# A decode step of cached attention and a gMLP: K transposed by the vector engine instead of the tensor engine, with other layouts for P, O and the weights

## The chip, the cores and the metric

The kernel runs on one core of a Trainium2 chip. The metric is the device time of one execution in microseconds; less is better. Before the change the median of three runs is 678.7 us (677.94 to 678.73). Profiled executions have a span that is a little shorter than the timed run (676.9 us for this one).

## The reference

One decode step with a batch of 4. The input row is normalised; its query attends to a cache of 4,096 keys and values in 32 heads of 128; beside it a gMLP branch works on the same normalised row; all is summed.

```python
B, Sq, D = (4, 1, 640)
H, Sk, Dh = (32, 4096, 128)
q = (x @ wq).reshape(B, Sq, H, Dh)                 # transposed to b h q d
scores = einsum('bhqd,bhkd->bhqk', q, k_cache) * Dh ** (-0.5)
p = softmax(scores)
o = einsum('bhqk,bhkd->bhqd', p, v_cache)
A = o.reshape(B, Sq, H * Dh) @ wo
# B branch, F = 1728, Fh = 864
z = gelu(einsum('bsd,df->bsf', x, w_in))
z1, z2 = z[..., :Fh], layernorm(z[..., Fh:])
g = w_sp * z2 + b_sp                               # S = 1
Bb = (z1 * g) @ w_out
return x0 + A + Bb                                 # x = layernorm(x0)
```

All inputs are bf16. The two caches are 4 x 32 x 4096 x 128 elements each, 134 MB, and every byte is read once: with the weights 282.2 MB come from memory.

## The kernel before, in words

Heads are taken in eight groups of four (`HG = 4`, `NG = 8`). One group of one batch element is a unit, `u` for K and `v` for V, 32 of each (`NU`). A unit is a tile of 128 partitions x 16,384 bf16, 4 MB: partition (head e, block m of 32) holds 128 consecutive keys of 128 elements, so each partition's row is 32 KB in one piece. All unit tiles come from one pool, `kvpool`, with five buffers; the two halves of `wq` and the gMLP weights use buffers of the same pool. All loads are issued in order by SP (`load_unit` at L273, `load_wo` at L281), each as soon as its buffer is free, and a load that waits holds back those behind it.

The program is one loop over steps `s` (L429), four to a unit, so that a step is a quarter of a unit (`NCH = 4`). In step `s`:

- `emit_T` (L296) transposes a quarter of K unit `u = s // 4`. K is read as words of two bf16, and TensorE transposes 16 blocks of 128 x 128 such words as f32 against the identity (L303) into PSUM tiles `pst` (three buffers). ScalarE (L292) and VectorE (L294) take turns in copying a `pst` out to `kT`.
- `emit_S` (L310) multiplies the quarter transposed one step earlier: eight matmuls of 512 columns (L321), four 32-column groups of the array side by side, one for each head, with weights from a zero-padded copy of q (`QZ`) that puts each result on its own row of the tile `S`. After 16 steps `S` of a group is full.
- Then the softmax of the group: the row maximum through small vector steps (L327 to L338), exp on ScalarE (L341), a 32x32-block transpose of P by VectorE (L349), copies by GpSimd (POOL) into the zero-padded weights `Zb` (L362, `z_fill`), and the row sums (`norm`, L366).
- `emit_V` (L375) starts `VD = 18` steps after K of the same group: 32 matmuls a V unit (L386), again in four column groups, into the PSUM tile `O`. After each two units `O` goes to SBUF (`emit_O`, L391), f32 matmuls select each head's part (`emit_sel`, L399), and after the fourth unit the group is projected with its slice of `wo` (`emit_proj`, L407, L411) into `proj`, which holds the sum over the whole kernel and starts with the input row.

`wo` of a group is a tile of 128 partitions x 4 heads x 640; a row in memory is 640 bf16, 1,280 bytes. Its pool has one buffer, so the load for the next group waits for the projection. The gMLP weights are loaded at step 28, its matmuls run at step 34 (L204 to L267); `w_out` has rows of 1,280 bytes.

The last V unit is loaded in four pieces (`TAIL`), and treated apart (L457 to L481): the earlier batch elements of the last group are projected first (L470), then 128 matmuls with V as weights (L479) give the last batch element, which is projected in turn (L481). L484 converts the sum and two stores end the kernel.

Of the kernel before, what the change touches and what calls it, by code (L numbers as in the profile page):

```python
# [16 lines left out]
def kernel(  # L17
# [16 lines left out]

    nc = tc.nc
    P = 128
# [8 lines left out]
    KP = T // (2 * NCH)  # L45
    assert KP == 16 and M == 32
# [5 lines left out]
    FC = (Fh + P - 1) // P  # L52
    FL = Fh - (FC - 1) * P
# [11 lines left out]
    ppool = ctx.enter_context(tc.tile_pool(name="ppool", bufs=1))  # L65
    opool = ctx.enter_context(tc.tile_pool(name="opool", bufs=1))
    wopool = ctx.enter_context(tc.tile_pool(name="wopool", bufs=1))
    ps_t = ctx.enter_context(tc.tile_pool(name="ps_t", bufs=3, space=bass.MemoryType.PSUM))
    ps_s = ctx.enter_context(tc.tile_pool(name="ps_s", bufs=2, space=bass.MemoryType.PSUM))
    ps_o = ctx.enter_context(tc.tile_pool(name="ps_o", bufs=1, space=bass.MemoryType.PSUM))  # L70
    ps_m = ctx.enter_context(tc.tile_pool(name="ps_m", bufs=1, space=bass.MemoryType.PSUM))
    ps_j = ctx.enter_context(tc.tile_pool(name="ps_j", bufs=1, space=bass.MemoryType.PSUM))
# [16 lines left out]
    nc.sync.dma_start(out=x_bf[:], in_=x_flat)  # L89


# [18 lines left out]
    QL = 16 + G * 32 + 16  # L110
    QZ = []
    for i in range(2):
        qz = const.tile([P, 2, QL], BF16, name=f"QZ{i}")
        nc.gpsimd.memset(qz[:].rearrange("p a l -> p (a l)").bitcast(F32), 0.0)
        QZ.append(qz)

# [25 lines left out]

    I32 = const.tile([P, 32], F32)
# [3 lines left out]
    B4 = const.tile([P, B], F32)  # L147
    nc.vector.tensor_reduce(out=B4[:], in_=I32[:].rearrange("p (w b c) -> p b w c", w=2, c=NCH), axis=AX.XY, op=ALU.add)
    SelP = const.tile([P, HG, B], F32)
    nc.vector.memset(SelP[:], 0.0)  # L150
    for q in range(4):
        nc.vector.tensor_copy(out=SelP[32 * q:32 * q + 32, q, :], in_=B4[32 * q:32 * q + 32, :])

    Pm = const.tile([P, 2, 2, P // 2], BF16)
    for w in range(2):
        nc.vector.tensor_copy(out=Pm[:, :, w, :], in_=ident_bf[:].rearrange("p (k w) -> p w k", w=2))
# [6 lines left out]
    m1 = const.tile([P, 32], F32)  # L163
    nc.vector.memset(m1[:], 0.0)
# [3 lines left out]
    for hf in range(NH):  # L168
        nc.tensor.matmul(proj[32 * hf:32 * hf + 32, 0:NO2], lhsT=ident_bf[:B, 0:32],
                         rhs=x_bf[:, hf * NO2:(hf + 1) * NO2], start=True, stop=False)  # L170

# [8 lines left out]
    q2_ps = misc_ps([P, 2, H * B], F32)  # L180
    for w in range(2):
        nc.tensor.matmul(q2_ps[:, w, :], lhsT=Pm[:, w, :, :].rearrange("p a k -> p (a k)"), rhs=q_bf[:],
                         start=True, stop=True)
    q2 = const.tile([P, 2, H * B], BF16)
    nc.vector.tensor_copy(out=q2[:], in_=q2_ps[:])

    def fill_qz(g):
        qz = QZ[g % 2]
        for w in range(2):
            r0 = 64 * w  # L190
            nc.gpsimd.tensor_copy(  # L191
                out=qz[r0:r0 + 64, :, 16:16 + G * 32].rearrange("p a (i z) -> p a i z", z=32)[:, :, :, 16 * w],
                in_=q2[r0:r0 + 64, :, g * G:(g + 1) * G])


    gw = {}
    wsp_bf = const.tile([P, 1], BF16)
    bsp_bf = const.tile([P, 1], BF16)
    wsp_f = const.tile([P, 1], F32)
    bsp_f = const.tile([P, 1], F32)  # L200
    nc.gpsimd.dma_start(out=wsp_bf[:], in_=B_w_sp.rearrange("a b -> (a b)").to_broadcast((P, 1)))
    nc.gpsimd.dma_start(out=bsp_bf[:], in_=B_b_sp.to_broadcast((P, 1)))

    def load_gmlp_weights():  # L204
        wt = kv_tile("w_gmlp")
        n_in = DC * F2
        w_in = wt[:, 0:n_in].rearrange("p (c f) -> p c f", c=DC)
        nc.sync.dma_start(out=w_in, in_=B_w_in.rearrange("(p c) f -> p c f", c=DC))
        w_out = wt[:, n_in:n_in + FC * NOUT].rearrange("p (c n) -> p c n", c=FC)
        nf = (FC - 1) * P  # L210
        nc.sync.dma_start(out=w_out[:, 0:FC - 1, :], in_=B_w_out[0:nf, :].rearrange("(c p) n -> p c n", p=P))
        nc.sync.dma_start(out=w_out[:FL, FC - 1, :], in_=B_w_out[nf:Fh, :])
        gw["in"] = w_in
        gw["out"] = w_out

    def gmlp_branch():
        nc.vector.tensor_copy(out=wsp_f[:], in_=wsp_bf[:])
        nc.vector.tensor_copy(out=bsp_f[:], in_=bsp_bf[:])
        zT = const.tile([P, 2, FC, B], F32)
        nc.vector.memset(zT[:], 0.0)  # L220
        zT_ps = misc_ps([P, 2, FC, B], F32)
        for part in range(2):
            for fc in range(FC):
                n = P if fc < FC - 1 else FL
                for c in range(DC):
                    f0 = part * Fh + fc * P
                    nc.tensor.matmul(zT_ps[:n, part, fc, :], lhsT=gw["in"][:, c, f0:f0 + n],  # L227
                                     rhs=xnT[:, c, :], start=(c == 0), stop=(c == DC - 1))
        nc.scalar.activation(out=zT[:, :, 0:FC - 1, :], in_=zT_ps[:, :, 0:FC - 1, :], func=ACT.Gelu_apprx_tanh)
        nc.scalar.activation(out=zT[:FL, :, FC - 1, :], in_=zT_ps[:FL, :, FC - 1, :], func=ACT.Gelu_apprx_tanh)  # L230
        z1 = zT[:, 0, :, :]
        z2 = zT[:, 1, :, :]
        st_in = const.tile([P, 2, FC, B], F32)
        nc.vector.tensor_copy(out=st_in[:, 0], in_=z2)
        nc.vector.tensor_tensor(out=st_in[:, 1], in0=z2, in1=z2, op=ALU.mult)
        st_ps = misc_ps([P, 2, FC, B], F32)
        nc.tensor.matmul(st_ps[:].rearrange("p s c b -> p (s c b)"), lhsT=ones_f[:, :],
                         rhs=st_in[:].rearrange("p s c b -> p (s c b)"), start=True, stop=True)
        st = const.tile([P, 2, B], F32)
        nc.vector.tensor_reduce(out=st[:], in_=st_ps[:].rearrange("p s c b -> p s b c"), axis=AX.X, op=ALU.add)  # L240
        mean = const.tile([P, B], F32)
        nc.vector.tensor_scalar(out=mean[:], in0=st[:, 0, :], scalar1=1.0 / Fh, scalar2=None, op0=ALU.mult)
        msq = const.tile([P, B], F32)
        nc.vector.tensor_tensor(out=msq[:], in0=mean[:], in1=mean[:], op=ALU.mult)
        var = const.tile([P, B], F32)
        nc.vector.scalar_tensor_tensor(out=var[:], in0=st[:, 1, :], scalar=1.0 / Fh, in1=msq[:],
                                       op0=ALU.mult, op1=ALU.subtract)
        rs = const.tile([P, B], F32)
        nc.scalar.activation(out=rs[:], in_=var[:], func=ACT.Sqrt, bias=eps_t[:, 0:1], scale=1.0)
        nc.vector.reciprocal(out=rs[:], in_=rs[:])  # L250
        t1 = const.tile([P, FC, B], F32)
        nc.vector.tensor_tensor(out=t1[:], in0=z2, in1=mean[:, None, :].to_broadcast((P, FC, B)),
                                op=ALU.subtract)
        nc.vector.tensor_tensor(out=t1[:], in0=t1[:], in1=rs[:, None, :].to_broadcast((P, FC, B)),
                                op=ALU.mult)
        nc.vector.tensor_scalar(out=t1[:], in0=t1[:], scalar1=wsp_f[:, 0:1], scalar2=bsp_f[:, 0:1],
                                op0=ALU.mult, op1=ALU.add)
        uT = const.tile([P, FC, B], BF16)
        nc.vector.tensor_tensor(out=uT[:], in0=z1, in1=t1[:], op=ALU.mult)
        gw["uT"] = uT  # L260

    def gmlp_out():
        for fc in range(FC):
            n = P if fc < FC - 1 else FL
            for hf in range(NH):
                nc.tensor.matmul(proj[32 * hf:32 * hf + B, 0:NO2], lhsT=gw["uT"][:n, fc, :],
                                 rhs=gw["out"][:n, fc, hf * NO2:(hf + 1) * NO2], start=False, stop=False)  # L267


    wo_v = A_wo.rearrange("(h p) n -> p h n", p=P)  # L270
    state = {}
# [9 lines left out]
    def load_wo(g):  # L281
        wo_t = wopool.tile([P, HG, NOUT], BF16, tag="wo", name=f"wo{g}")
        nc.sync.dma_start(out=wo_t[:], in_=wo_v[:, g * HG:(g + 1) * HG, :])
        state[("wo", g)] = wo_t

    evac_ctr = [0]

    def evacuate(dst, src):
        k = evac_ctr[0] % 2
        evac_ctr[0] += 1  # L290
        if k:
            nc.scalar.copy(out=dst, in_=src)  # L292
        else:
            nc.vector.tensor_copy(out=dst, in_=src)  # L294

    def emit_T(u, ch):  # L296
        kw = state[("k", u)][:].bitcast(F32)
        kT = ktpool.tile([P, KP, HG, M, 2], BF16, tag="kT", name="kT")
        for pc in range(4):
            pst = ps_t.tile([P, 4, P], F32, tag="pst", name="pst")  # L300
            for e in range(4):
# [115 lines left out]
    def at(s, fn):  # L417
        sched.setdefault(s, []).append(fn)
# [98 lines left out]
```

## Time and profile before

| | before |
|---|---|
| time, median of 3 | 678.7 us |
| span of the profiled run | 676.9 us |
| PE busy | 501.5 us (74%) |
| of it K transposes, L303 | 313.1 us |
| ACT busy, of it copies of K, L292 | 275.0 us, 254.9 us |
| DVE busy, of it copies of K, L294 | 218.4 us, 176.9 us |
| bytes read, mean rate | 282.24 MB, 417 GB/s |
| a 4 MB tile of K, issue to landing | 43.6 us |

The busy times are sums over an engine's instructions; engines run side by side, so they don't add up. The page cuts the span into 40 slices and gives for each the busy share of an engine in tenths, the share of the DMA engines and the rate. The time from issue to landing is long because several tiles are queued at a time: it is a queue's length, not a transfer's.

### The profile page before, as it was taken

How to read it: one execution, taken by the hardware profiler on the slowest of the kernel's cores; microseconds unless marked ns; L12 is line 12 of the kernel's file. 1: busy time of each engine (PE TensorE's matmuls, PEld its weight loads, DVE VectorE, ACT ScalarE, POOL GpSimd, SP SyncE). 2: the span in 40 equal slices, each digit the busy share in tenths (PEclk: the TensorE clock that was granted, in tenths of full speed). 3: DMA queues.
4: the chain of work that ended last, by engine and by line, in shares of the span. 5: the costliest groups of instructions: out<-in, count | busy, mean ns of one | idle time of the engine just before them, and what ended most of it. 6: DMA issues, size and time to landing. Idle time of an engine off the chain costs nothing.

```text
span 676.9 us, 10603 instructions
## 1 busy us (share of the span) xinstructions
PE 501.5 (74%) x4663; PEld 356.0 (53%) x4663; DVE 218.4 (32%) x398; ACT 275.0 (41%) x291; POOL 33.5 (5%) x92
## 2 busy tenths in 40 slices
PE   0699898669766797677687787688876789766846
PEld 0566566446544565555465556456654556554424
DVE  4144542243222433223233242233332243322300
ACT  0176764364423544334344333344442444433300
POOL 1000200010000010002000020000100010000100
PEclk9999998788878989688898878987787998967865
DMA  8999999999999999999999999999999999999994
GB/s 324 431 429 429 433 423 429 407 430 432 416 429 431 431 433 417 429 434 431 429 419 433 427 431 428 422 433 432 429 417 431 431 429 433 423 425 432 409 417 171
DMA packets 15333, 282.92 MB, mean 418 GB/s; under 512 B 1356, under 2 KB 6328, under 8 KB 6584
## 3 DMA queue, kind: packets, MB, share of 16 engines
q1 hardware_dynamic: 15216, 282.25, 98.0%
q8 instruction: 36, 0.59, 0.4%
q14 instruction: 9, 0.07, 0.0%
q0 software_dynamic: 64, 0.00, 0.0%
q10 hardware_dynamic: 8, 0.00, 0.0%
HBM read 282.24 MB, written 0.01 MB: 417 GB/s over the span
## 4 chain that ended last, share of the span: by engine, by line
DMA 58%; PE 32%; ACT 6%; DVE 3%; issue 1%; SPq 0%; ACTq 0%; DVEq 0%
DMA k<-in_A_k_cache_dram 55%; PE pst L303 19%; PE S L321 5%; ACT kT L292 4%; PE O L386 3%; DMA v<-in_A_v_cache_dram 3%; PE misc L403 1%; PE proj L411 1%; DVE kT L294 1%; ACT p_bf L341 1%; PE ol L479 1%; DVE m L327 1%; DVE x L349 0%; PE misc L368 0%; PE misc L227 0%
## 5 line engine op out<-in xcount | busy, mean ns | idle before, releaser
L292 ACT COPY kT<-pst 128x1024 bf16<-128x1024 bf16 x256 | 254.9, 1013 | 325.9 <-PE pst L303 243.3
L303 PE MATMUL pst<-ident_f,k 128*128 128x128 f32 x2048 | 313.1, 310 | 99.9 <-DMA k<-in_A_k_cache_dram 95.2
L303 PEld LDWEIGHTS pst<-ident_f,k 128*128 128x128 f32 x2048 | 265.9, 160 | 164.0 <-issue 122.2
L294 DVE COPY kT<-pst 128x1024 bf16<-128x1024 bf16 x256 | 176.9, 692 | 334.9 <-PE pst L303 321.1
L321 PE MATMUL S<-kT,QZ 128*32 128x512 bf16 x1024 | 95.2, 385 | 13.0 <-ACT kT L292 9.9
L386 PE MATMUL O<-v,Zb 128*32 128x512 bf16 x992 | 67.4, 411 | 10.1 <-DMA v<-in_A_v_cache_dram 10.1
L386 PEld LDWEIGHTS <-Zb 128*32 128x32 bf16 x992 | 31.0, 101 | 39.0 <-issue 15.3
L321 PEld LDWEIGHTS <-QZ 128*32 128x32 bf16 x1024 | 20.9, 94 | 49.8 <-issue 38.0
L362 POOL COPY Zb<-x 32x256 bf16<-32x256 bf16 x64 | 25.2, 394 | 184.0 <-DVE ds L351 153.5
L403 PE MATMUL misc<-I,O_sb 128*128 128x8 f32 x120 | 20.2, 296 | 9.4 <-DVE O_sb L294 6.3
L403 PEld LDWEIGHTS misc<-I,O_sb 128*128 128x128 f32 x120 | 19.0, 241 | 14.8 <-DVE O_sb L294 10.7
L191 POOL COPY QZ<-q 64x32 bf16<-64x32 bf16 x16 | 5.1, 320 | 422.6 <-PE S L321 402.4
L294 DVE COPY O_sb<-O 128x512 f32<-128x512 f32 x8 | 5.5, 692 | 36.8 <-PE O L386 36.8
L368 PE MATMUL misc<-ds,ones_f 128*128 128x16 f32 x16 | 3.6, 302 | 13.6 <-DVE ds L351 13.3
L462 ACT COPY O_sb<-O 128x512 f32<-128x512 f32 x1 | 0.6, 585 | 28.0 <-PE O L386 28.0
L341 ACT ACTIVATE p_bf<-S,negmax 128x512 bf16<-128x512 f32 x8 | 5.5, 687 | 15.9 <-DVE negmax L338 15.8
L368 PEld LDWEIGHTS misc<-ds,ones_f 128*128 128x128 f32 x16 | 2.9, 225 | 16.8 <-DVE ds L351 16.3
L404 DVE TENSOR_TENSOR oT<-misc,rinv 128x8 bf16<-128x8 f32 x15 | 2.5, 167 | 28.0 <-PE misc L403 28.0
L176 PE MATMUL misc<-xnT,wq 128*128 128x4 bf16 x160 | 4.6, 166 | 8.2 <-DMA wq<-in_A_wq_dram 4.5
L411 PE MATMUL proj<-wo,oT 128*4 128x320 bf16 x64 | 8.8, 420 | 2.1 <-DVE oT L404 1.8
L176 PEld LDWEIGHTS <-wq 128*128 128x128 bf16 x160 | 4.4, 104 | 8.4 <-DMA wq<-in_A_wq_dram 8.4
L349 DVE STREAM_TRANSPOSE x<-p_bf 128x512 bf16<-128x512 bf16 x8 | 5.7, 712 | 9.7 <-ACT p_bf L341 9.7
(88 smaller groups left out, 74.5 us busy)
## 6 DMA issues: line engine op xcount, KB each, us to landing
k<-in_A_k_cache_dram SPq DMA_DIRECT2D x32, 4096.0 KB, 43.6
v<-in_A_v_cache_dram SPq DMA_DIRECT2D x31, 4096.0 KB, 37.5
wo<-in_A_wo_dram SPq DMA_DIRECT2D x8, 640.0 KB, 29.3
wq<-in_A_wq_dram SPq DMA_DIRECT2D x1, 3072.0 KB
w_gmlp<-in_B_w_in_dram SPq DMA_DIRECT2D x1, 2160.0 KB, 31.8
wq<-in_A_wq_dram SPq DMA_DIRECT2D x1, 2048.0 KB
v<-in_A_v_cache_dram SPq DMA_DIRECT2D x1, 2048.0 KB, 23.5
v<-in_A_v_cache_dram SPq DMA_DIRECT2D x1, 1024.0 KB, 25.5
```

Of the source, the lines that this page charges most:

```text
L176: nc.tensor.matmul(q_ps[:, h, :], lhsT=wq_t[c][:, h * Dh:(h + 1) * Dh], rhs=xnT[:, c, :], start=(c == 0), stop=(c == DC - 1))
L292: nc.scalar.copy(out=dst, in_=src)
L294: nc.vector.tensor_copy(out=dst, in_=src)
L303: nc.tensor.transpose(pst[:, e, :], kw[:, k * P:(k + 1) * P], ident_f[:])
L321: nc.tensor.matmul(S_ps[32 * hd:32 * hd + 32, :, :], lhsT=qz[:, w, w0:w0 + 32], rhs=kT[:, :, hd, :, w], start=(b == 0 and ch == 0 and w == 0),
L327: nc.vector.tensor_reduce(out=m1[:, 0:1], in_=S_ps[:].rearrange("p k m -> p (k m)"), axis=AX.X, op=ALU.max)
L341: nc.scalar.activation(out=p_bf[:].rearrange("p k m -> p (k m)"), in_=S_ps[:].rearrange("p k m -> p (k m)"), func=ACT.Exp, bias=negmax[:, ...
L362: nc.gpsimd.tensor_copy(out=dst, in_=x[r0:r0 + 32, :, 2 * bb:2 * bb + 2, :])
L386: nc.tensor.matmul(O_ps[32 * q:32 * q + 32, :, :], lhsT=Zb[bb][:, w0:w0 + 32], rhs=vv[:, e, :, :], start=(b1 == 0 and e < 4), stop=((b1 == ...
L403: nc.tensor.matmul(oh[:], lhsT=O_sb[:, j, :], rhs=SelO[:, j, :, :], start=(j == 0), stop=(j == 3))
L411: nc.tensor.matmul(proj[32 * hf:32 * hf + B, 0:NO2], lhsT=oT[:, hd, :], rhs=wo_t[:, hd, hf * NO2:(hf + 1) * NO2], start=False, stop=(last ...
L479: nc.tensor.matmul(ol_ps[:], lhsT=vv[:, t, :], rhs=zc, start=(t == 0), stop=(t == T - 1))
```

## The change

Its purpose is to take the transposes of K from TensorE and their copies from ScalarE and VectorE, and to give loads longer rows. The parts:

1. K: VectorE's own transpose, which turns each 32 x 32 block of 4-byte words on its own, from SBUF to SBUF (`emit_T`). `kT` holds other pieces of the key dimension on each block of 32 partitions, so that `emit_S` has four matmuls for each of two column groups, and q is brought to a matching layout (`Pm`, `q3`, `fill_qz`).
2. P: the maximum is spread by an f32 matmul with ones; exp writes each value four times; 16 TensorE transposes bring P into PSUM; ScalarE fills `Zb` from there (GpSimd before).
3. O: always copied by ScalarE; selected once a group, with eight f32 matmuls that have O as the moving operand, a mask and four small matmuls (`emit_sel`, `emit_oT`). The last group keeps the old way and is projected once, at the end.
4. `wo` of the first seven groups is read with the four rows of a partition in one piece (5,120 bytes), and loaded seven steps later; groups 5 and 6 in three pieces by partitions. The last group's `wo` keeps its rows, comes in three pieces, and is issued just ahead of the last V tile.
5. The gMLP weights are the first load and the gMLP is computed before q. `w_out` lies on 108 partitions with eight rows of 640 in one piece each. The input row is loaded from ScalarE's queue.

```diff
+    wg = kv_tile("w_gmlp")
+    nc.sync.dma_start(out=w_in, in_=B_w_in.rearrange("(p c) f -> p c f", c=DC))
+    w_out = wg[:FP, n_in:n_in + FC * NOUT].rearrange("p (c n) -> p c n", c=FC)
+    nc.sync.dma_start(out=w_out, in_=B_w_out.rearrange("(p c) n -> p c n", c=FC))
...
+    wo_q = A_wo.rearrange("(g p c) n -> g p c n", p=P, c=HG)
...
     def emit_T(u, ch):
         kw = state[("k", u)][:].bitcast(F32)
-        kT = ktpool.tile([P, KP, HG, M, 2], BF16, tag="kT", name="kT")
-        for pc in range(4):
-            pst = ps_t.tile([P, 4, P], F32, tag="pst", name="pst")
-            for e in range(4):
-                k = ch * KP + pc * 4 + e
-                nc.tensor.transpose(pst[:, e, :], kw[:, k * P:(k + 1) * P], ident_f[:])
-            evacuate(kT[:, pc * 4:(pc + 1) * 4].rearrange("p e h m w -> p (e h m w)"),
-                     pst[:].rearrange("p e m -> p (e m)").bitcast(BF16))
+        n = TC * KW
+        kT = ktpool.tile([P, n], F32, tag="kT", name="kT")
+        nc.vector.transpose(kT[:], kw[:, ch * n:(ch + 1) * n])
...
-        for w in range(2):
-            for hd in range(HG):
-                w0 = 16 + (hd * B + b) * 32 - (b * NCH + ch)
-                nc.tensor.matmul(S_ps[32 * hd:32 * hd + 32, :, :], lhsT=qz[:, w, w0:w0 + 32],
-                                 rhs=kT[:, :, hd, :, w], start=(b == 0 and ch == 0 and w == 0),
-                                 stop=(b == B - 1 and ch == NCH - 1 and w == 1))
+        for kw in range(4):
+            for i in range(2):
+                q = 2 * (ch % 2) + i
+                nc.tensor.matmul(S_ps[32 * q:32 * q + 32, :, :], lhsT=qz[:, b, kw, w0:w0 + 32],
+                                 rhs=kT[:, i, :, kw // 2, :, kw % 2], start=(b == 0 and c2 == 0 and kw == 0),
+                                 stop=(b == B - 1 and c2 == 1 and kw == 3))
...
+            p_i = opool.tile([P, 8, HG, M], BF16, tag="O_sb", name="p", bufs=3)
+            nc.scalar.activation(out=p_i[:], in_=S_ps[:, 8 * i:8 * i + 8, None, :].to_broadcast((P, 8, HG, M)),
+                                 func=ACT.Exp, bias=negmax[:, 0:1], scale=scale, accum_out=rs2[:, i:i + 1])
...
-        nc.vector.transpose(x[:].rearrange("p e b c -> p (e b c)"), p_bf[:].rearrange("p k m -> p (k m)"))
+        for t in range(16):
+            nc.tensor.transpose(x[:, t, :], p_bf[t // 8][:, t % 8].rearrange("p h m -> p (h m)"), IdP[:])
...
-            nc.gpsimd.tensor_copy(out=dst, in_=x[r0:r0 + 32, :, 2 * bb:2 * bb + 2, :])
+                nc.scalar.copy(out=dst, in_=src[:, 2 * bb + b1])
...
+    WO_CUTS = {NG - 3: (0, 112, 120, 128), NG - 2: (0, 112, 124, 128)}
...
-        at(NCH * B * g + VD + 4, lambda g=g: load_wo(g))
+        at(min(NCH * B * g + VD + 11, NCH * (NU - 1) + VD), lambda g=g: load_wo(g, WO_CUTS.get(g, (0, P))))
```

## The prediction

> **What bounds the kernel now.** I read the page's occupancy first, then the DMA queues, then the stretches of the span, and the chain of waits last. The 40 slices say which resource never rests:
>
> ```profile
> PE 501.5 (74%) x4663; PEld 356.0 (53%) x4663; DVE 218.4 (32%) x398; ACT 275.0 (41%) x291; POOL 33.5 (5%) x92
> DMA  8999999999999999999999999999999999999994
> DMA packets 15333, 282.92 MB, mean 418 GB/s; under 512 B 1356, under 2 KB 6328, under 8 KB 6584
> q1 hardware_dynamic: 15216, 282.25, 98.0%
> q8 instruction: 36, 0.59, 0.4%
> ```
>
> No compute engine is full; the DMA engines are at nine tenths or more in every slice but the first and the last. The chain of waits gives PE 32% of the span and the L303 transposes 19%, which invites the reading that PE is half the bound. It isn't: in the first 90 us PE runs nearly without a break and the DMA share is still 1.0, because five tiles of `kvpool` let the queue run ahead. So the removal of PE transposes is worth nothing by itself; what counts is bytes times rate, plus the head, plus the tail. Stretches of 10 us (PE, PEld, DVE, ACT, POOL busy; then clock, DMA share, GB/s):
>
> ```profile
> 30.00:40.00 10.00, 10.00 (x74) 8.28 (x72) 4.82 (x8) 6.93 (x7) 0.00 (x0) 1.00 1.02 437
> 130.00:140.00 10.00, 10.00 (x71) 7.58 (x70) 4.79 (x7) 6.32 (x8) 0.00 (x0) 0.85 1.06 398
> 180.00:190.00 10.00, 9.45 (x95) 6.63 (x97) 4.48 (x7) 7.08 (x7) 0.00 (x0) 0.96 1.00 411
> 500.00:510.00 10.00, 9.77 (x83) 7.41 (x82) 5.27 (x8) 7.46 (x8) 0.00 (x0) 0.91 0.98 406
> 590.00:600.00 10.00, 2.88 (x35) 2.06 (x28) 0.88 (x3) 0.00 (x0) 0.00 (x0) 0.69 1.02 439
> ```
>
> The rate is the same with PE full (437) and PE mostly idle (439). It falls only where rows of 1,280 bytes pass: 130 to 140 holds `w_out` of the gMLP, the other two hold a `wo`. The mean of the undisturbed middle is about 428 GB/s, so one K or V tile (4096 KB = 4.194 MB) takes 9.80 us. The tail:
>
> ```profile
> 640.00:641.00 1.00, 0.90 (x12) 0.50 (x16) 0.04 (x1) 0.00 (x0) 0.74 (x2) 0.50 0.69 295
> 641.00:642.00 1.00, 1.00 (x16) 0.41 (x12) 0.00 (x0) 0.00 (x0) 0.00 (x0) 0.50 0.53 229
> 666.00:667.00 1.00, 1.00 (x6) 1.00 (x6) 0.00 (x0) 0.00 (x0) 0.00 (x0) 0.50 0.49 201
> ...
> 661.06 3.60 PE L386 MATMUL O<-v,Zb 128*32 128x512 bf16 x32 [5.32 <-DMA v<-in_A_v_cache_dram]
> 667.54 1.23 PE L411 MATMUL proj<-wo,oT 128*4 128x320 bf16 x8 [0.26 <-DVE oT L468]
> 668.70 3.57 PE L479 MATMUL ol<-Zb,v 128*128 128x4 bf16 x128
> 673.80 0.48 DVE L484 CAST o_bf<-proj 64x320 bf16<-64x320 f32 x1 [1.33 <-PE proj L411]
> ```
>
> Three losses show. At 640 to 642 the queue was nearly dry, since SP had waited up to 29.7 us for L411 to free the single `wo` buffer (the waits of the DMA queue). From 665 to 669.5 only half of the engines move data (share 0.40 to 0.57, nothing after). And the last PE work runs from V30's landing at 661.06 without a DMA wait to 672.27, some 2.5 us after the transfers stopped.
>
> [...] 712 ns for 512 elements (L349) and 212 ns for 32 (L329, f32) are 1.04 ns per element. A long f32 one isn't shown. [...] No view shows single engines. [...] matmuls into different 32-column groups run together; here eight S matmuls of 385 ns take 0.55 us at full clock, so four at a time do.
>
> **The change part by part.**
>
> K transposes. Out go 2048 PE transposes (313.1 us), 256 ACT copies (254.9) and 256 DVE copies (176.9); in come 128 DVE transposes of 128x2048 f32. From the slope: 0.212 + 2016 x 1.04 ns = 2.31 us each, 296 us in all. If 4-byte words cost two cycles it is 0.212 + 2016 x 2.08 ns = 4.4 us, 563 us. I take 2.31[...]. Need: in the K-only start a chunk arrives every 9.80/4 = 2.45 us, later every 4.9 us. At 2.31 (2.4 with gaps) DVE keeps pace even with the start; before, units 0 to 4 took 61 us, 12.2 us each, and the DMA did not notice. On the path: 0.
>
> S. Still eight matmuls per chunk, but two column groups alternate in place of four: four rounds of about 0.22 us at full clock, 0.43 at the half clock that idle stretches show, so 0.9 to 1.7 us per chunk; with V's 0.45 to 0.9, at most 2.6 of 4.9 us. If pairs did not overlap it were 3.4 + 0.9 = 4.3 us. Hidden behind the transfers either way.
>
> Softmax, Z fill, O. The chain gets longer: two exps of 1024 elements (0.69 us for 512 now, so about 1.1 each), 16 PE transposes, eight ACT copies of about 0.3 us in place of four POOL copies of 0.39, three more DVE steps. About 8 us from the maximum to Z in place of 4.5. In that time V's first matmuls and all behind them on PE wait, and ACT holds O's eviction behind the Z copies; the buffers absorb 8 us (K lands 43.6 us after issue, four tiles deep). O selection per group: 8 f32 matmuls per group for 16. All hidden, 0.
>
> Rows of 5 KB. Deficit of a window with a `wo`: (428-411)/428 x 10 = 0.40 us, 0.51 for 406. About 0.46 x 7 = 3.2 us if all comes back; [...]the eighth `wo` keeps 1,280-byte rows. I take 2.5 (range 1.5 to 3.2).
>
> gMLP first. Its row deficit was (428-398)/428 x 10 = 0.7 us[...] Net 0[...]. The order itself hides: K0 lands some 5 us later, but bytes are only reordered; K2's buffer is free near 28 us while K0 and K1 keep the queue busy to about 43. `x_bf` moves to the ACT queue: the first big load is issued 0.4 us earlier.
>
> Wo later. SP now waits for the projection behind V30, not V29, so the 640 dip (0.31 + 0.47 = 0.8 us) goes.
>
> Tail. The last group is projected once (8 matmuls, 1.23 us gone), and V31 now ends after `wo`, 1.6 us after V30 plus its own 9.8. PE's chain from V30 (3.6 + 0.6 + 1.9 + 0.2, then 3.1 us for 112 of 128 L479) is done before the last piece lands. So the end is last landing + 0.45 + 0.2 + 1.25 + 0.5 + the store of 2.6 = 5.0 us plus waits, against 676.9 - 669.5 = 7.4 now. I take 1.7 us.
>
> Balance. The half of the engines that lags carries about 4.5 us more. Instruction fetch is one suspect: 0.4% of 16 engines is 2.7 us on each, 5.4 if only eight carry it. [...] Perfect balance gives 4.5/2 = 2.2 us, none gives 0[...]. I take 1.2.
>
> Sum: 2.5 + 0 + 0.4 + 0.8 + 1.7 + 1.2 = 6.6 us. 678.7 - 6.6 = 672.1, rounded to 672.
>
> **The rivals.**
> A. The balance does not come and 5 KB rows give the low end: 1.5 + 0.4 + 0.8 + 1.0 = 3.7 us, 675.0. For it: nothing here shows which engines lag. Against: the `wo` dips are plain.
> B. All comes back and the engines end together: 3.2 + 0.4 + 0.8 + 2.2 + 2.2 = 8.8, 669.9; with both head gaps gone too (share 0.12 and 0.30 from 7 to 9 us) 668.3. For it: the share of 0.5 in the tail. Against: the head gap is unexplained.
> C. The f32 transpose is at half rate. At 4.4 + 0.1 us per chunk a unit takes 18 us, the five buffers run out between K6 and the first V tiles, and following tile by tile with five buffers the queue idles about 16 us; 672 + 16 = 688. After that 18 plus a softmax is just under the 19.6 us of a K and a V. [...]
> D. Nothing: [...]678.
>
> **How the numbers follow.** Main forecast 0.42, A 0.22, B 0.18, C 0.11, D 0.07. The range is 666.5 to 678: it holds the main case, A and B with the ends of their terms, and half of D; C stays out. Faster needs less than 677.3: the first three, 0.82; within 0.2%: most of D, 0.05; slower: C and the rest of D, 0.13.
>
> **What would show it.** Right: 128 f32 transposes near 2.3 us and DVE near 340 us busy; ACT below 80; DMA share still 0.98 or more; no dips below 415 GB/s in the middle; no dip before the last `wo`; the last PE work waiting for V31 and the end about 5.5 us after it. Wrong: a transpose of 4 us or more, a DMA share under 0.9 between 60 and 130 us (C); half the engines still moving for 4 us at the end (A); a rate in the middle other than 428, which I hold to be a property of the transfers and not of PE's traffic.

## The result, and the profile after

The change made the kernel slower: 684.25 us median (681.85 to 685.0, four runs) against 678.32 us for the kernel before in the same session (677.93 to 678.73), a ratio of 1.0081 with a 95% interval of 1.0055 to 1.0108. The profiled execution has a span of 682.6 us. The forecast of 672.0 us was wrong in direction, and the time lies above its range.

The page of the kernel after, its occupancy, DMA queues and the line of the K transposes (instruction count, tile, number | busy us, mean ns | idle time before, what ended it):

```profile
PE 341.2 (50%) x2793; PEld 152.4 (22%) x2793; DVE 318.9 (47%) x251; ACT 60.3 (9%) x183; POOL 10.2 (1%) x42
DMA  8999999999999999999999999999999999999994
GB/s 255 437 430 429 429 431 432 428 434 429 434 429 430 430 430 433 432 425 431 433 433 422 431 433 434 431 426 429 432 435 432 322 431 429 430 423 316 432 418 185
DMA packets 11916, 282.66 MB, mean 414 GB/s; under 512 B 1400, under 2 KB 1924, under 8 KB 3076
q1 hardware_dynamic: 11808, 282.25, 98.3%
q8 instruction: 22, 0.36, 0.2%
L305 DVE STREAM_TRANSPOSE kT<-k 128x2048 f32<-128x2048 f32 x128 | 284.2, 2279 | 213.8 <-DMA k<-in_A_k_cache_dram 211.4
```

All compute engines are well under full, the bytes are the same, and the DMA engines are as busy as before (98.3%, 98.0% before). Yet the mean rate fell from 418 to 414 GB/s. The slices of 17 us say where: 255 at the start (324 before), 322 and 316 late. All other slices before the last dip are 422 to 437. The engines are busy and move less, so here their packets are slower (2,038 ns against 1,215, below), and their idle time is not longer. Stretches of 10 us of the same kernel show it (PE, PEld, DVE, ACT, POOL busy; then clock, DMA share, GB/s):

```profile
10.00:20.00 10.00, 1.85 (x14) 2.04 (x14) 4.67 (x11) 1.58 (x2) 0.00 (x0) 1.00 0.98 303
520.00:530.00 10.00, 6.99 (x58) 2.91 (x56) 5.04 (x3) 0.00 (x0) 0.00 (x0) 0.75 0.98 421
530.00:540.00 10.00, 0.00 (x0) 0.00 (x0) 0.48 (x1) 0.00 (x0) 0.00 (x0) 0.59 1.03 257
540.00:550.00 10.00, 5.81 (x32) 1.62 (x31) 8.81 (x5) 0.00 (x0) 0.00 (x0) 0.73 0.99 416
610.00:620.00 10.00, 2.80 (x40) 1.95 (x40) 0.30 (x1) 0.00 (x0) 0.00 (x0) 0.86 1.03 319
620.00:630.00 10.00, 2.23 (x10) 0.61 (x12) 4.90 (x3) 0.00 (x0) 0.00 (x0) 0.50 1.00 342
```

At 530 to 540 the DMA share is 1.03 and the rate 257; PE has nothing to do, for its next tile is late. Against 428 GB/s the five late stretches lack 0.16 + 4.0 + 0.3 + 2.5 + 2.0 = 9.0 us of transfer. The timeline of SP's queue names what was in it (start, duration, load, number of pieces):

```profile
493.22 1.13 SPq L295 DMA_DIRECT2D wo<-in_A_wo_dram  x3
...
575.42 1.20 SPq L295 DMA_DIRECT2D wo<-in_A_wo_dram  x3
```

These are the two `wo` in three pieces (`WO_CUTS`). A K tile lands a median of 46.8 us after its issue, so they pass at about 535 and 620 us, in the two dips. The dip of 10 to 20 us is where `w_out` on 108 partitions passes (its packets run from 8.6 to 16.1 us). The single packets that the trace keeps, which no view prints, say the same from below: a 32 KB packet of a K or V tile takes a median of 1,215 ns from 500 to 520 us and 2,038 ns from 530 to 540; a 5,120-byte packet of `wo` takes 199 ns in the five loads that are not cut and 340 ns in the two that are. So the cut load is slow, and so are the tiles that pass beside it. The end of the chain of waits, and then three stretches of the tail (columns as above):

```profile
610.33 45.85 DMA v<-in_A_v_cache_dram
656.19 21.38 DMA v<-in_A_v_cache_dram
677.62 0.60 PE ol L520 x16
678.47 1.25 PE proj L447 x8
679.74 0.48 DVE o_bf L525
```

```profile
672.00:673.00 1.00, 0.52 (x14) 0.42 (x15) 0.17 (x1) 0.00 (x0) 0.00 (x0) 0.50 0.55 225
674.00:675.00 1.00, 0.52 (x20) 0.43 (x17) 0.00 (x0) 0.00 (x0) 0.00 (x0) 0.50 0.35 143
676.00:677.00 1.00, 0.71 (x21) 0.54 (x18) 0.00 (x0) 0.00 (x0) 0.00 (x0) 0.50 0.08 33
```

The last PE work now follows the last landing of V31 at 677.6, and the span ends 5.0 us later. The trickle is still there: a DMA share of 0.55 at 672 us, 0.35 at 674, 0.08 at 676.

### The profile page after: what moved, and what is told of

Read it like the earlier page. It is cut to its first block, busy times and chain, and to the rows that moved or that the text cites. A ratio compares the mean times of both kernels' runs of the same rounds, so it can differ in the third digit from the quotient of the medians.

```text
span 682.6 us, 6424 instructions
## 1 busy us (share of the span) xinstructions
PE 341.2 (50%) x2793; PEld 152.4 (22%) x2793; DVE 318.9 (47%) x251; ACT 60.3 (9%) x183; POOL 10.2 (1%) x42
## 3 DMA queue, kind: packets, MB, share of 16 engines
q1 hardware_dynamic: 11808, 282.25, 98.3%
## 4 chain that ended last, share of the span: by engine, by line
DMA 56%; PE 15%; issue 13%; DVE 13%; ACT 3%; POOL 0%; DVEq 0%; ACTq 0%; POOLq 0%
DMA k<-in_A_k_cache_dram 44%; DMA v<-in_A_v_cache_dram 10%; DVE kT L305 9%; PE O L409 5%; PE S L323 3%; PE zT_ps L212 2%; ACT p L351 2%; DMA bsp_bf<-in_B_b_sp_dram 2%; PE misc L426 1%; PE x L364 1%; DVE m L330 1%; PE misc L253 1%; DVE om L429 1%; PE misc L334 1%; ACT O_sb L417 0%
## 5 line engine op out<-in xcount | busy, mean ns | idle before, releaser
L305 DVE STREAM_TRANSPOSE kT<-k 128x2048 f32<-128x2048 f32 x128 | 284.2, 2279 | 213.8 <-DMA k<-in_A_k_cache_dram 211.4
L323 PE MATMUL S<-kT,QZ 128*32 128x512 bf16 x1024 | 195.4, 520 | 266.2 <-DVE kT L305 263.8
L323 PEld LDWEIGHTS <-QZ 128*32 128x32 bf16 x1024 | 55.9, 112 | 402.4 <-issue 387.3
L409 PE MATMUL O<-v,Zb 128*32 128x512 bf16 x992 | 88.0, 451 | 8.4 <-DMA v<-in_A_v_cache_dram 8.4
L351 ACT ACTIVATE p<-S,negmax 128x1024 bf16<-128x1024 f32 x16 | 17.7, 1110 | 282.3 <-DVE negmax L345 282.3
L375 ACT COPY Zb<-x 32x128 bf16<-32x128 bf16 x128 | 27.3, 254 | 10.2 <-PE x L364 9.5
L364 PE MATMUL x<-IdP,p 128*128 128x128 bf16 x128 | 16.1, 305 | 18.9 <-ACT p L351 18.6
L426 PE MATMUL misc<-O_sb,SelG 128*16 128x128 f32 x112 | 18.7, 314 | 3.7 <-ACT O_sb L417 1.5
L212 PEld LDWEIGHTS <-w_gmlp 128*108 128x108 bf16 x80 | 16.0, 294 | 0.1
L212 PE MATMUL zT_ps<-xnT,w_gmlp 128*108 128x4 bf16 x80 | 15.9, 336 | 0.3 <-DVE xnT L142 0.3
L426 PEld LDWEIGHTS misc<-O_sb,SelG 128*16 128x16 f32 x112 | 11.0, 108 | 10.3 <-ACT O_sb L417 4.0
## 6 DMA issues: line engine op xcount, KB each, us to landing
k<-in_A_k_cache_dram SPq DMA_DIRECT2D x32, 4096.0 KB, 46.8
```

The source lines that it names most:

```text
L212: nc.tensor.matmul(zT_ps[:, part, fc, :], lhsT=w[:, c, fc, :], rhs=xnT[:, c, :], start=(c == 0), stop=(c == DC - 1))
L305: nc.vector.transpose(kT[:], kw[:, ch * n:(ch + 1) * n])
L323: nc.tensor.matmul(S_ps[32 * q:32 * q + 32, :, :], lhsT=qz[:, b, kw, w0:w0 + 32], rhs=kT[:, i, :, kw // 2, :, kw % 2], start=(b == 0 and c ...
L351: nc.scalar.activation(out=p_i[:], in_=S_ps[:, 8 * i:8 * i + 8, None, :].to_broadcast((P, 8, HG, M)), func=ACT.Exp, bias=negmax[:, 0:1], s ...
L364: nc.tensor.transpose(x[:, t, :], p_bf[t // 8][:, t % 8].rearrange("p h m -> p (h m)"), IdP[:])
L375: nc.scalar.copy(out=dst, in_=src[:, 2 * bb + b1])
```

## The experiments

The theory formed from these views: a load that covers fewer than 128 partitions (its height, below; such a load is called low) is slow, and makes the transfers of its time slow (P or P1 in the expectations). The rivals: the cut loads use too few engines or load some of them more (balance, the prediction's own idea; P2); more and smaller transfers cost, whatever their shape; the vector transposes disturb the transfers. Ratios below are to the kernel before in the same session, with 95% intervals. Its median was 677.97 to 678.70 us in the four sessions, so a difference between runs of two sessions is good to some 0.7 us.

**1. The cuts of `wo` undone.**

```diff
-    WO_CUTS = {NG - 3: (0, 112, 120, 128), NG - 2: (0, 112, 124, 128)}
+    WO_CUTS = {}
```

> The changed kernel with every wo of groups 0 to 6 in one load of 128 partitions; nothing else differs. Theory P (loads of fewer than 128 partitions are slow, and slow the tiles in flight with them): the two stretches at 257 and at 319 to 342 GB/s lost (430-257)/430 x 10 = 4.0 us and (111+88)/430 x 10 = 4.6 us, so 8.6 us come back: 684.25 - 8.6 = 675.6 us, and no stretch of 10 us in the middle lies below 415 GB/s. Rival C (the vector transposes or the S matmuls hold up the transfers): the dips stay, 684 us. Rival W (5 KB rows are slow in themselves): small dips at every wo, and no gain, 683 to 684.

Measured: 675.77 us, 0.996 [0.9947, 0.9973]: 8.5 us less than the changed kernel, close to the 9.0 read from the windows. The slices of this run have the late dips gone, the one at the start not:

```profile
GB/s 251 434 424 426 433 435 434 428 427 429 436 436 425 432 427 431 436 428 429 431 430 434 431 425 434 435 426 432 431 431 434 423 432 431 434 431 428 429 417 181
```

The cuts alone turn a kernel a little faster than the one before into a slower one.

**2. The cuts in two pieces.** 112 and 16 partitions, two counts that the author assumed to give every engine the same bytes. No view shows whether they do.

```diff
-    WO_CUTS = {NG - 3: (0, 112, 120, 128), NG - 2: (0, 112, 124, 128)}
+    WO_CUTS = {NG - 3: (0, 112, 128), NG - 2: (0, 112, 128)}
```

> The changed kernel with groups 5 and 6 of wo in two pieces, 112 and 16 partitions[...]. Theory P1[...]: the dips stay, about 257 to 340 GB/s for 10 us each, 682 to 685 us. Theory P2 (what is slow is that a few engines get more than others and run out of step): the dips go, 675.6 us as without cuts.

Measured: 684.89 us, 1.01 [1.0085, 1.0115], as slow as the changed kernel. The stretches where the two loads pass:

```profile
530.00:540.00 10.00, 0.00 (x0) 0.00 (x0) 0.00 (x0) 0.00 (x0) 0.00 (x0) 0.61 1.04 277
620.00:630.00 10.00, 2.34 (x12) 0.66 (x14) 5.01 (x3) 0.00 (x0) 0.00 (x0) 0.50 0.96 331
```

So the loss needs no piece of 4, 8 or 12 partitions. That an uneven share of bytes isn't the cause either rests on the author's assumption alone.

**3. `w_out` on 96 partitions.** On top of 1.

```diff
-    FC = next(c for c in range(1, Fh + 1) if Fh % c == 0 and Fh // c <= P)
+    FC = next(c for c in range(1, Fh + 1) if Fh % c == 0 and Fh // c <= P and Fh // c % 16 == 0)
```

> No cuts of wo, and w_out on 96 partitions with nine rows each in place of 108 with eight[...]. The first 20 us moved 5.6 MB where the kernel before moved 6.8 MB, 2.9 us of transfers. Theory P2: the head comes back, 2 to 3 us less than without cuts alone, 672.7 us[...]. Theory P1: 96 partitions are still less than 128, so the head stays slow, within 1 us of the kernel without cuts, 675 to 676 us.

**4. `w_out` on 128 partitions**, six rows in one piece each, and a second small load of the 96 rows that remain; the gMLP's matmuls and tiles follow the new split (`...`). On top of 1.

```diff
...
-    nc.sync.dma_start(out=w_out, in_=B_w_out.rearrange("(p c) n -> p c n", c=FC))
+    nf = (FC - 1) * P
+    nc.sync.dma_start(out=w_out[:, 0:FC - 1, :], in_=B_w_out[0:nf, :].rearrange("(p c) n -> p c n", c=FC - 1))
+    nc.sync.dma_start(out=w_out[:FL, FC - 1, :], in_=B_w_out[nf:Fh, :])
...
```

> No cuts of wo, and w_out as 128 partitions with six rows each in one piece (960 KB) and a rest of 96 rows of 1,280 bytes (120 KB). Both P1 and P2: the head comes back, 2 to 3 us less than without cuts alone, 672.7 us, and the stretch from 10 to 20 us is above 400 GB/s in place of 303. Rival H (the slow head is the order of the loads, or the small loads of w_sp and b_sp, and not the shape of w_out): no change, 675.6 us.

Measured: 674.44 us, 0.9946 [0.9929, 0.9963] for 3, and 669.44 us, 0.987 [0.9855, 0.9884] for 4. The same stretch at the start in runs 1, 3 and 4, one fence each:

```profile
10.00:20.00 10.00, 2.06 (x15) 2.25 (x15) 4.67 (x11) 1.58 (x2) 0.00 (x0) 1.00 1.00 303
```

```profile
10.00:20.00 10.00, 2.87 (x21) 3.03 (x21) 4.66 (x11) 1.58 (x2) 0.00 (x0) 1.00 1.02 330
```

```profile
10.00:20.00 10.00, 3.84 (x74) 3.88 (x75) 4.58 (x11) 1.58 (x2) 0.00 (x0) 1.00 1.03 414
```

108 partitions 303 GB/s, 96 partitions 330, 128 partitions 414. The step from 108 to 96 gives 1.3 us, a little more than height alone was expected to give and less than balance was, if 96 partitions are the balanced load that the author took them for, which is not shown; run 4 gives 6.3, over twice the 2 to 3 expected. Of those 6.3 us the windows show (414 - 303) / 428 x 10 = 2.6 at the start, while `w_out` passes. Another 2.6 lie between 20 and 640 us, after it has landed: there run 4 moves 268.09 MB and run 1 266.97. The last 1.1 is left for the end. The part in the middle comes with the edit (266.95 MB in run 3; 268.12 and 268.04 in runs 9 and 10, which are built on run 4), but no low load is in flight then, and run 4 changes the rows' length and the gMLP's tiles along with the height. Its cause is open.

**5. Rows of 5 KB alone.** The kernel before, with `wo` of all eight groups read as the change does (so its rows no longer meet their own heads: the right output projection is left out, its work stays).

```diff
...
-        nc.sync.dma_start(out=wo_t[:], in_=wo_v[:, g * HG:(g + 1) * HG, :])
+        nc.sync.dma_start(out=wo_t[:], in_=wo_q[g])
```

> The kernel before with one edit: each partition of wo takes four neighbouring rows in one piece of 5 KB (all eight groups). The rows then meet the wrong elements of O, so this kernel leaves the right output projection out and only its time counts. The prediction's term: 2.5 us for seven loads is 0.36 us each, so 2.9 us for eight, 675.4 us; from 2 to 3.7 us, 674.6 to 676.3. Rival: rows make no difference to the end, since other losses take their place, 678 us.

Measured: 676.55 us, 0.9972 [0.9962, 0.9983], 1.4 us less by the medians and 1.2 to 2.6 by the interval. Three stretches of the run:

```profile
130.00:140.00 10.00, 10.00 (x79) 7.15 (x77) 4.89 (x8) 6.85 (x8) 0.00 (x0) 0.92 1.05 394
180.00:190.00 10.00, 9.45 (x79) 7.26 (x81) 4.59 (x7) 7.08 (x7) 0.00 (x0) 0.86 1.01 431
500.00:510.00 10.00, 9.23 (x93) 6.50 (x96) 4.85 (x7) 7.46 (x8) 0.00 (x0) 0.98 1.00 427
```

The windows of `wo` rose from 411 and 406 to 431 and 427, as forecast; that of the gMLP, which this run leaves alone, did not. But eight such dips at 0.46 us are 3.7 us, and the time fell by 1.4: what two windows of 10 us show can't be multiplied by eight.

**6. The vector transposes alone.** The kernel before with K transposed by VectorE, the PE transposes and copies gone; `emit_S` then reads blocks that it wasn't written for, so the scores are left out in effect while its work stays.

```diff
...
-                nc.tensor.transpose(pst[:, e, :], kw[:, k * P:(k + 1) * P], ident_f[:])
-            evacuate(kT[:, pc * 4:(pc + 1) * 4].rearrange("p e h m w -> p (e h m w)"),
-                     pst[:].rearrange("p e m -> p (e m)").bitcast(BF16))
+        n = KP * P
+        nc.vector.transpose(kT[:].rearrange("p k h m w -> p (k h m w)").bitcast(F32), kw[:, ch * n:(ch + 1) * n])
```

> The kernel before with one edit: each quarter of K is transposed by one vector transpose of 128x2048 f32 into kT, and the 16 PE transposes with their four copies are gone; S, then, is made of other elements, so the scores are left out and only the time counts. The prediction's term for this part: 0, so 677.5 to 679 us; at most the dry queue near the end (0.8 us) goes. Rival C: the transposes by PE and the copies by ACT and DVE were in the way of the transfers, so the time falls by more than 2 us, below 676.3. Rival D: the vector transposes slow the transfers, above 680.

Measured: 675.52 us, 0.9958 [0.9945, 0.997]: 2.5 us less. The expected 0 missed, and the time lies below rival C's 676.3. The vector transposes do not disturb the transfers; something is gained with the PE transposes and their copies gone, and run 12 asks what. Its tail, and its instruction queue, stand beside those of run 12 below.

**7. The cut at 64.** On top of 4: `wo` of the same two groups in two halves of 64 partitions.

```diff
-    WO_CUTS = {}
+    WO_CUTS = {NG - 3: (0, 64, 128), NG - 2: (0, 64, 128)}
```

> The kernel with w_out on 128 partitions (669.4 us), and wo of groups 5 and 6 in two halves of 64 partitions. [...] P1: dips for these two groups again, smaller or as large as with 112 and 16, so 672 to 678 us. Rival P3 (only counts that are no power of two, or no multiple of 32, are slow): no dip, 669.4 us.

**8. The cut in the kernel before**, without any vector transpose and with rows of 1,280 bytes.

```diff
-        nc.sync.dma_start(out=wo_t[:], in_=wo_v[:, g * HG:(g + 1) * HG, :])
+        cuts = (0, 112, 128) if g in (NG - 3, NG - 2) else (0, P)
+        for p0, p1 in zip(cuts[:-1], cuts[1:]):
+            nc.sync.dma_start(out=wo_t[p0:p1], in_=wo_v[p0:p1, g * HG:(g + 1) * HG, :])
```

> The kernel before with wo of groups 5 and 6 in two pieces of 112 and 16 partitions, rows of 1,280 bytes as they were. P1: the cut alone costs about 4 us a group here too, 683 to 688 us, with two stretches of 10 us below 350 GB/s, though PE transposes K. Rival: the cut is slow only beside the vector transposes or only with long rows, 678 to 679 us.

**10. The same number of pieces, cut by columns.** On top of 4: two loads of 128 partitions and two rows each in place of one.

```diff
-            for p0, p1 in zip(cuts[:-1], cuts[1:]):
-                nc.sync.dma_start(out=wo_t[p0:p1], in_=wo_q[g, p0:p1])
+            cc = (0, 2, HG) if g in (NG - 3, NG - 2) else (0, HG)
+            for c0, c1 in zip(cc[:-1], cc[1:]):
+                nc.sync.dma_start(out=wo_t[:, c0:c1, :], in_=wo_q[g, :, c0:c1, :])
```

> The kernel with w_out on 128 partitions, and wo of groups 5 and 6 in two loads as in the cut at 64, but cut by columns: each load has all 128 partitions, with pieces of 2,560 bytes. P1: nothing happens, 669.0 to 670.0 us and no dip, against the 678.85 us of the cut at 64 partitions. Rival Q (two loads in place of one, or one more wait in SP's queue, cost the 4 to 5 us a group): 678 us and dips.

Measured: 678.85 us for 7, 1.0013 [1.0002, 1.0024], 9.4 us above run 4, with a wider spread than the others (677.28 to 682.9 in 20 runs). 688.26 us for 8, 1.0149 [1.0134, 1.0165], 10.3 us above the kernel before. 669.3 us for 10, 0.9864 [0.985, 0.9877], no more than run 4. The stretches where the two loads pass, of 7, of 8 and of 10:

```profile
530.00:540.00 10.00, 3.48 (x16) 0.93 (x16) 6.15 (x3) 0.00 (x0) 0.00 (x0) 0.50 0.99 332
...
610.00:620.00 10.00, 0.00 (x0) 0.00 (x0) 0.69 (x1) 0.00 (x0) 0.00 (x0) 0.61 1.00 247
```

```profile
500.00:510.00 10.00, 9.68 (x83) 7.26 (x82) 5.26 (x8) 7.60 (x8) 0.00 (x0) 0.93 1.01 279
510.00:520.00 10.00, 3.59 (x48) 2.01 (x47) 0.86 (x2) 0.41 (x1) 0.00 (x0) 0.93 1.01 352
...
590.00:600.00 10.00, 8.42 (x94) 5.27 (x92) 3.64 (x7) 4.12 (x5) 0.00 (x0) 1.00 1.03 316
```

```profile
530.00:540.00 10.00, 6.55 (x30) 1.78 (x31) 8.89 (x4) 0.00 (x0) 0.00 (x0) 0.50 1.04 445
...
610.00:620.00 10.00, 5.31 (x30) 1.62 (x31) 8.89 (x4) 0.00 (x0) 0.00 (x0) 0.69 1.01 434
```

Read together: a cut by partitions costs 4 to 5 us each, at 112/16 and at 64/64, with rows of 5 KB and of 1,280 bytes, with vector transposes and without. A cut by columns costs nothing. So it is neither the number of loads, nor their row length, nor the transposes: it is that each load covers fewer than 128 partitions.

**9. `w_out` with no low load at all.** On top of 4: the second load takes the last 128 rows; the activations that meet the 32 rows which came already are set to zero (`...`).

```diff
-    nc.sync.dma_start(out=w_out[:FL, FC - 1, :], in_=B_w_out[nf:Fh, :])
+    nc.sync.dma_start(out=w_out[:, FC - 1, :], in_=B_w_out[Fh - P:Fh, :])
...
```

> The kernel with w_out on 128 partitions, and its rest taken as the last 128 rows in place of the last 96: 32 rows come twice, and their activations are set to zero the second time. No load but the input row is then on fewer than 128 partitions. P1: the rest of the dip in the stretch from 10 to 20 us (414 GB/s against 436 before) goes, 0.3 to 1 us less: 668.4 to 669.1. Rival: that dip is the eighth part of the weights in rows of 1,280 bytes, or noise, no change, 669.4 us.

Measured: 669.04 us, 0.9861 [0.9847, 0.9874]. The same stretch at the start:

```profile
10.00:20.00 10.00, 3.20 (x68) 3.24 (x69) 4.58 (x11) 1.58 (x2) 0.00 (x0) 1.00 1.02 433
```

414 became 433, the full rate, though this load reads 41 KB more; in time it is 0.4 us, within what these runs can tell. Runs 4, 9 and 10 are the fastest kernels of this study.

**11. Instructions put back, first try.** Run 6 with 16 matmuls of one column a quarter on constant operands, their result thrown away (scores left out as in 6): do the 2.5 us of run 6 come from fewer instructions being fetched?

```diff
...
+        idle = ps_t.tile([P, 16], F32, tag="idle", name="idle")
+        for e in range(16):
+            nc.tensor.matmul(idle[:, e:e + 1], lhsT=ident_bf[:], rhs=ident_bf[:, e:e + 1], start=True, stop=True)
```

> The kernel before with vector transposes of K (675.5 us), and 16 idle matmuls of one column a quarter, so that PE has as many instructions as the kernel before again: the instruction queue goes from 0.33 back to about 0.59 MB, while PE stays mostly idle and nothing waits for these matmuls. The scores are left out as there. Theory I (fewer instructions to fetch, carried by engines that finish last, gave most of the 2.5 us): 676.6 to 677.8 us. Rival J (it was the earlier issue of wo near the end, or the head): no change, 675.5 us.

Measured: 714.55 us, 1.0531 [1.0517, 1.0546]. It decides nothing between the two theories, for it made a bound of its own. Nothing held these matmuls back, so the program's order ran most of them early, ahead of q and of the first S:

```profile
70.00:80.00 10.00, 9.22 (x248) 7.50 (x246) 2.31 (x1) 0.00 (x0) 0.00 (x0) 1.00 0.01 3
```

248 matmuls in 10 us, one K transpose, and 3 GB/s: with S late, `kT` stays taken (VectorE waits up to 27.5 us for S), K's tiles don't come free, and SP has no buffer to load into (it waits up to 43.0 us for a K transpose). It shows on the way what a late S would have cost.

**12. Instructions put back, second try.** The added matmuls read the fresh `kT`, so that none can run ahead, and start with the ninth unit.

```diff
...
+        if u >= 2 * B:
+            idle = ps_t.tile([P, 20], F32, tag="idle", name="idle")
+            for e in range(20):
+                nc.tensor.matmul(idle[:, e:e + 1], lhsT=ident_bf[:], rhs=kT[:, e % KP, e % HG, 0:1, 0], start=True, stop=True)
```

> The kernel with K transposed by the vector engine alone (scores left out as in the run it is built on, 675.5 us) with 20 matmuls of one column a quarter of a unit put back on PE from the ninth unit on, each reading the fresh kT, so that none can run ahead; their result is thrown away. 24 x 4 x 20 = 1920 instructions bring PE's count near that of the kernel before; PE stays under full. Theory I, that fetching instructions costs the 2.5 us which the transposes alone gave: the instruction queue goes back to 0.5 MB or more and the time to 677.5 to 678.5 us. Theory J, that the 2.5 us come from the earlier projections (the load of wo no longer late near 640 us) and from the start: the instruction queue goes up and the time stays at 675 to 676 us. If the instruction queue stays at 0.33 MB the run says only that PE's extra work is hidden.

Measured: 677.95 us, 0.9996 [0.9988, 1.0004]: all of run 6's gain is gone. The instruction queue and four stretches of the tail, of 6 and then of 12:

```profile
q8 instruction: 20, 0.33, 0.2%
```

```profile
662.00:663.00 1.00, 0.49 (x3) 0.49 (x3) 0.00 (x0) 0.45 (x1) 0.00 (x0) 0.50 0.72 295
664.00:665.00 1.00, 0.74 (x6) 0.50 (x8) 0.17 (x1) 0.00 (x0) 0.00 (x0) 0.50 0.53 213
666.00:667.00 1.00, 1.00 (x44) 1.00 (x42) 0.00 (x0) 0.00 (x0) 0.00 (x0) 0.50 0.19 78
668.00:669.00 1.00, 1.00 (x44) 1.00 (x42) 0.00 (x0) 0.00 (x0) 0.00 (x0) 0.50 0.00 0
```

```profile
q8 instruction: 35, 0.57, 0.3%
```

```profile
662.00:663.00 1.00, 1.00 (x16) 0.36 (x8) 0.00 (x0) 0.00 (x0) 0.00 (x0) 0.50 0.76 315
664.00:665.00 1.00, 0.60 (x8) 0.00 (x0) 0.00 (x0) 0.30 (x1) 0.00 (x0) 0.50 0.55 229
666.00:667.00 1.00, 1.00 (x6) 1.00 (x6) 0.00 (x0) 0.00 (x0) 0.00 (x0) 0.50 0.50 201
668.00:669.00 1.00, 1.00 (x19) 0.46 (x16) 0.00 (x0) 0.00 (x0) 0.00 (x0) 0.50 0.37 147
```

PE is busy for 337 of 677 us (279 in run 6), so its work is hidden. What changed is the DMA: the same bytes end some 3 us later, and the plateau at half share is longer (0.50 at 666 us and 0.37 at 668, against 0.19 and 0.00 in run 6). 1,920 matmuls with as many weight loads, 0.24 MB on the instruction queue, cost 2.4 us. The earlier issue of `wo` doesn't explain run 6: run 12 keeps most of it (636.50 us, 633.96 in run 6, 641.37 before) and has no gain. Spread over all engines 0.24 MB at 428 GB/s would be 0.6 us, an estimate. Why it is four times that is not shown: no view tells which engine fetches, and no run has the fetches without the 58 us of added work on PE. So that the fetches are the cause is argued.

## Why the prediction was wrong

**The step that failed** is the pricing of the loads of less than 128 partitions, in the terms "gMLP first" and "Balance": `w_out` on 108 partitions was put at a net 0, and the cuts of `wo` at a gain, within the 1.2 us. Both were the author's estimates of bytes per engine, and how these loads deal their bytes out to the engines is not shown. What the runs show instead is that such loads are slow themselves and slow what passes beside them, at a DMA share of 0.96 to 1.04: the cuts cost 8.5 us (run 1) and the shape of `w_out` 6.3 us (run 4; 2.6 of them while it passes), 14.8 in all. Without them the change gives 678.48 - 669.44 = 9.0 us; with them it loses 5.9. That run 4 lands near rival B's 669.9 is luck: B has 3.2 us from the rows, of which the runs show 1.2, and 2.2 from balance, which no run shows. Run 10 kept the number of loads of run 7 and took the loss away. Whether run 2 evened out the bytes per engine is not shown, so balance is not ruled out as the way in which height acts.

A sign stood in the profile before. The deepest of its three dips, 398 GB/s at 130 to 140 us, was put down to rows of 1,280 bytes like the other two, but the last 96 rows of `w_out` pass there as a load of 96 partitions. Packets of 32 KB that start between 130 and 135 us take a median of 1,504 ns; beside the `wo` of full height at 180 and 500 us they take 1,216. It is no proof, for rows of `w_out` at full height pass at the same time, but the prediction didn't ask for the difference.

Why height matters is not shown: no view and no run here tells which engine carries a row. What is shown is that both sides are slow: in the changed kernel a packet of `wo` takes 340 ns in the cut loads and 199 in the others, and one of a tile beside a cut load 2,038 ns in place of 1,215.

**K transposes.** The mechanism was right: 2,279 ns each where 2,310 was forecast, DVE 318.9 us busy for about 340, ACT 60.3 for under 80, a DMA share of 98.3%, and no lack of tiles in the K-only start, so rival C fell. The cost "on the path: 0" was mis-sized: run 6 gives 2.5 us for them alone, and run 12 takes it back with added matmuls whose result nothing reads. The prediction took 437 against 439 GB/s in two windows as a sign that PE's work doesn't touch the rate; but 2.5 us in 676 are 1.6 GB/s in 428, too little for a window of 10 us. It had named instruction fetch a suspect for the lagging half of the engines (before, eight packets are in flight most of the time from 666 to 669 us, where there are 16 at 200), and did not put the two thousand transposes' own fetch into the sum.

**Rows of 5 KB.** The dips went as forecast, the gain was mis-sized: 1.4 us for eight groups (run 5), some 1.2 for seven, where 2.5 was taken. By run 5's interval seven groups give 1.0 to 2.3, so the low end of 1.5 may hold and 2.5 does not.

**The dry queue near 640 us.** It is gone, but the 0.8 us did not follow on its own: in run 12 `wo` is issued at 636.50 in place of 641.37, and the time is that of the kernel before.

**Tail.** Right: the span ends 5.0 us after the last landing, where 5.0 plus waits was forecast, and the last PE work waits for V31.

**The head.** The 0.4 us doesn't show: the first 20 us move 6.82 MB before (246 and 436 GB/s), 5.58 after, 6.68 in run 4 (254 and 414) and 6.88 in run 9 (255 and 433).

**The remainder.** Of the 9.0 us of run 4, the removed transposes give 2.5, rows 1.2 and the tail 1.7 if its forecast holds, if they add up; 3.6 us were not taken apart, among them the gMLP's place at the start, the new O selection and the last `wo`. Where most of the gain lies can be said: between 20 and 640 us run 4 moves 268.09 MB and the kernel before 265.28, worth 6.6 us at 428 GB/s. (The O selection has no fewer f32 matmuls than before: the trace counts 16 a group in both, where the prediction set 8 against 16. Its term was 0 either way.)

## What to carry to other kernels

In a kernel bound by DMA like this one, keep every load at the full 128 partitions: a cut by partitions cost 4 to 5 us each here. Where a load must be split, split it by columns, which cost nothing (run 10). Bring a ragged weight in at full height, with a small rest or with rows read twice (runs 4 and 9, 0.4 us apart), rather than lower the height of all of it. Price a load not by its bytes and its engines alone: look whether the trace has one of that height, and how fast the tiles beside it are; if it has none, give the range room for it. Engine instructions off the critical path were not free here either: they come over DMA queues too (`q8 instruction`, 0.33 MB in run 6 and 0.57 in run 12), and 3,840 of them went with 2.4 us. Fewer, larger instructions may be worth something even on an engine with slack: 2.5 us in run 6.

## What the hardware did that was not expected

- A `wo` of 0.66 MB, 1.5 us of the full rate, costs 4 to 5 us more when it comes as two or three loads by partitions, with a DMA share of 0.96 to 1.04 and 247 to 332 GB/s in its worst 10 us. The packets of the tiles beside it take some 1.7 times as long (2,038 against 1,215 ns in the changed kernel).
- The DMA share gives no warning of it: 1.03 stands beside 257 GB/s and beside 414 GB/s alike.
- 1,920 small matmuls on a half-idle PE, with their weight loads 0.24 MB of instructions, cost 2.4 us of 676.
- A long vector transpose of f32, 128 x 2048 from SBUF to SBUF, takes 2,279 ns, 1.11 ns per word of four bytes. The bf16 one of 512 elements takes 712 ns, 1.39 ns each, so words of four bytes show no half rate.
